# Late weight conversions on ScalarE: first steps kept in the order of the calls, more places for words, two conversions called later

## The chip, the core and the metric

The kernel runs on one core of a Trainium2 chip. Five engines work side by side, each on a queue of its own that it takes in order: PE (TensorE, the matmuls), DVE (VectorE), ACT (ScalarE), POOL (GpSimd) and SP (SyncE, which here issues all DMAs). The metric is the device time of one execution in microseconds (us). Three runs of the kernel before gave 495.65, 496.67 and 497.83; the median is 496.67.

## What is computed

A windowed attention over 2 x 768 tokens (8 heads of 64), a feed-forward block with a softmax-weighted activation and a norm, and a second feed-forward block with ELU:

```python
h = x @ w_in                               # x: attention output, 1536 x 512; w_in 512 x 1024
e = np.exp(h - np.max(h, axis=-1, keepdims=True))
solu = h * e / (np.sum(e, axis=-1, keepdims=True) + 1e-09)
mu, var = solu.mean(-1, keepdims=True), solu.var(-1, keepdims=True)
x = ((solu - mu) / np.sqrt(var + 1e-06) * g_ln) @ w_out

h = x @ w_in2                              # 512 x 2048
g = np.where(h > 0.0, h, np.exp(np.minimum(h, 0.0)) - 1.0)
out = g @ w_out2                           # 2048 x 512
```

The four weights reach the core as 64-bit floats.

## The kernel before

**Conversions.** A weight tile of 128 rows by 512 columns arrives as words (512 KB, 32-bit halves) and is made float32 by `to_f32`: a first step on ACT (line 120, the absolute value of the high halves), one on POOL (line 123), and three on DVE (lines 124, 125 and 129, the last of which also reads the low halves and so frees the place of the words). `convert` adds the split of each number into a high part (ACT, line 133) and a remainder (DVE, line 100), since each product is made of three matmuls on the parts (`mm3x`, lines 103 to 105). The weights w_in2 and w_out2 are the late ones, here called w3 and w4: 16 tiles each, in the order of the list `todo` (w3 0, w3 1, w4 0, w3 2, w3 3, w4 1, w3 4, w3 5, w4 2, w4 3, w3 6, w4 4, w3 7, w4 5, w3 8, w4 6, w3 9, w4 7 ...). A w3 tile stays in SBUF; a w4 tile is split, stored to DRAM (line 364, tensor `w4d`) and loaded again three times as `w4r`. The profile drops the digit of a tensor's name: words of w3 show as `in_w_in`, words of w4 as `in_w_out`, like those of the first block's weights.

**Places for words.** Words lie where results will come later. `y[0..2]`, the output of the first block (512 tokens each), serve as `stage[0..2]`, with two places each: the place h of `stage[2]` is the columns d = 2h and 2h + 1 of `y[2]`. The late words use the two places of `stage[2]` (the list `spare`) until the second call of the first loop over d below, and then four places in tiles `yc` and `yd`, which take over the room of w_in. `fetch` loads words while fewer than len(spare) - 1 are waiting. `more_w` is one late conversion: it calls `fetch`, stores the w4 tile that was converted last, and converts the oldest words.

**Ticks.** After an opening, the work runs in 24 ticks. Tick t issues the scores of query tile t + 6 (`attn_s`), a half row of h (`mm_in`), the transposes of tile t + 4 (`attn_p`), transposes (`tr`) and output products (`mm_out`) of the first block as they come due, and the values of tile t + 3 (`attn_x`: product `x_ps`, then the copy xT on ACT, line 252, and its remainder on DVE). The last `x_ps` is in tick 20. Then come late conversions: one in each of the ticks 11 to 20, two in 21, 22 and 23. `mm_out(i, d)` is the product for third i of the tokens and 128 output columns d; it is copied to y by ACT (line 305), in two pieces where a third crosses two tiles of y. Third 1 (ticks 17 to 20) is the first that writes y[1], third 2 the first that writes y[2]. `lnT` (lines 290 and 100) is the transposed, normalized activation, made from the transposes `t_ps`.

**The turn.** Two loops over d follow, with the products of thirds 2 and 3, the last transposes and more conversions: one in each of the last two calls of the first loop and in each call of the second. Then the second block starts; its first loop makes the remaining conversions. All these products share a PSUM pool of four places (`psb`).

**What sets the order.** SP's queue is in the order of the calls (`manual_schedule`, line 448); before a DMA, it waits until the place it writes is free, and everything called later waits behind it. On the other engines a planner orders the instructions by its own estimate of when each can run, and an instruction whose inputs it takes as landed can be put ahead of earlier calls. `keep_in_program_order` (line 122) forbids this for one instruction: it is queued after the instruction called just before it on its engine. The keyword `pin` of `to_f32` asks for that. In the kernel before, only the conversions of w_out ask for it (line 158).

Of the kernel before, what the change touches and what calls it, by code (L numbers as in the profile page):

```python
# [12 lines left out]
I32 = mybir.dt.int32  # L13
# [38 lines left out]
def tile_kernel(ctx: ExitStack, tc: tile.TileContext, qd, kT, v, w_in, w_out, g_ln, w_in2, w_out2,  # L52
# [4 lines left out]
    state = {"late": 0}  # L57
# [10 lines left out]
    stage = [[t.bitcast(I32)[:, i * 1024:(i + 1) * 1024].rearrange("p (k f) -> p k f", k=KD)  # L68
              for i in range(KD * TC // 1024)] for t in flat]
# [41 lines left out]
    def load_words(bits, src):  # L111
        nc.sync.dma_start(bits, src if len(src.shape) == 3 else src.rearrange("p (k f) -> p k f", k=KD))


    def to_f32(bits, outs=None, pin=False):
        words = bits.rearrange("p k (f two) -> p k f two", two=2)
        low, high = words[:, :, :, 0], words[:, :, :, 1]
        a = p_k.tile([128, KD, 128], I32, tag="conv", name="conv", bufs=3)
        x = a.bitcast(F32)
        first = nc.scalar.activation(x, high.bitcast(F32), AF.Abs)  # L120
        if pin:
            tc.keep_in_program_order(first)
        nc.gpsimd.tensor_scalar(x, x, F64_HUGE, F64_TINY, op0=ALU.min, op1=ALU.max)  # L123
        nc.vector.tensor_scalar(a, a, 3, 0x3FFFFFF8, op0=ALU.logical_shift_left, op1=ALU.bitwise_and)  # L124
        nc.vector.scalar_tensor_tensor(a, high, -0x40000000, a, op0=ALU.bitwise_and, op1=ALU.bitwise_or)
        to = a if outs is None else outs
        if outs is not None:
            low, a = (t.rearrange("p (h k) f -> p h (k f)", h=2) for t in (low, a))
        nc.vector.scalar_tensor_tensor(to, low, 29, a, op0=ALU.logical_shift_right, op1=ALU.bitwise_or)
        return x  # L130

    def split(hi, lo, x):
        nc.scalar.activation(hi, x, AF.Copy)  # L133
        lo_of(lo, x, hi)

    def convert(bits, src, hi, lo, g=None, pin=False):
        if src is not None:
            load_words(bits, src)
        hi, lo = (t if len(t.shape) == 3 else t.rearrange("p (k f) -> p k f", k=KD) for t in (hi, lo))
        x = to_f32(bits, pin=pin)  # L140
        if g is None:
            split(hi, lo, x)
        else:
            nc.scalar.activation(hi, x, AF.Copy, scale=g)
            nc.vector.scalar_tensor_tensor(lo, x, g, hi.bitcast(F32), op0=ALU.mult, op1=ALU.subtract)
# [17 lines left out]
    def load_k(b):  # L163
        k_sb[b] = p_k.tile([128, NP, S + 2 * PAD], F32, tag="k", name="k_sb", bufs=2)
        for p in range(NP):
            nc.sync.dma_start(k_sb[b][:, p, :], kT[b, p])

    def sum_k(b):
        ksum[b] = p_at.tile([128, NP, NB], F32, name="ksum") if b else kws[0][:, :, WIN:KW]
        for p in range(NP):  # L170
            nc.vector.tensor_reduce(
                ksum[b][:, p, :], k_sb[b][:, p, PAD:PAD + S].rearrange("d (n j) -> d n j", j=BLOCK),
                axis=AX.X, op=ALU.max)


    def sum_v(b):
        pst = psb.tile([128, DM], F32, tag="b", name="vs_ps")
        v_sb = p_k.tile([128, NP, S + 2 * PAD], F32, tag="k", name="v_sb", bufs=2).rearrange("p a s -> p (a s)")
        for i in range(S // 128):
            vt = v_sb[:, i * DM:(i + 1) * DM]  # L180
            nc.sync.dma_start(vt, v[b, PAD + i * 128:PAD + (i + 1) * 128, :])
            c0 = NB - i * 4
            nc.tensor.matmul(pst, lhsT=avg[:, c0:c0 + 128], rhs=vt, start=i == 0, stop=i == S // 128 - 1)
        vsum[b] = p_at.tile([128, DM], F32, tag="vsum", name="vsum", bufs=1)
        nc.scalar.activation(vsum[b][WIN:KW, :], pst[WIN:KW, :], AF.Copy)
# [121 lines left out]
                t0 = t1  # L307

    w3t, w3e, w3l, w3_hl, w4s, w4_hl, yhl, yf = {}, {}, {}, {}, {}, {}, {}, {}
    stores, ahead, spare = [], [], [*stage[2]]  # L310
    todo = [("w3", 0), ("w3", 1), ("w4", 0), ("w3", 2), ("w3", 3), ("w4", 1), ("w3", 4), ("w3", 5), ("w4", 2),
            ("w4", 3), ("w3", 6), ("w4", 4), ("w3", 7), ("w4", 5), ("w3", 8), ("w4", 6), ("w3", 9), ("w4", 7),
            ("w4", 8), ("w4", 9), ("w3", 10), ("w3", 11)]
# [3 lines left out]
    def fetch():  # L317
        while todo and len(ahead) < len(spare) - 1:
            what, f = todo.pop(0)
            b = spare[state["late"] % len(spare)]  # L320
            state["late"] += 1
            if what == "w3":
                load_words(b, w_in2[:, f * 128:(f + 1) * 128].bitcast(I32).rearrange("(k p) f -> p k f", p=128))
            else:
                load_words(b, w_out2[f * 128:(f + 1) * 128, :].bitcast(I32))
            ahead.append((what, f, b))

    def home(p):
        if p < 2:
            t = w3t[p] = p_k.tile([128, 3200], F32, tag="k", bufs=2, name="w3f")  # L330
            w4s[p] = t[:, 1792:2816].rearrange("p (c f) -> p c f", c=2)
        elif p == 2:
            w3t[p] = p_k.tile([128, 2048], F32, tag="f2", name="w3f")
        elif p > 4:
            w3t[p] = p_w.tile([128, 2048], F32, tag=f"w{p - 5}", name="w3f")

    def w3f(p):
        return w3t[p][:, :1792].rearrange("p (s f) -> p s f", s=7)

    def base_of(f):  # L340
        return w3f(f // 2)[:, 2:6:3] if f % 2 else w3f(f // 2)[:, 0:4:3]

    def convert_w3(f, b):
        if f % 2 == 0:
            home(f // 2)
        to_f32(b, base_of(f).bitcast(I32))

    def sums_w3(p):
        t = w3f(p)
# [5 lines left out]
    def convert_w4(f, b):  # L355
        t = w4s[f % 2]
        tr_ = t.bitcast(F32R)
        convert(b, None, tr_[:, 0], tr_[:, 1])
        stores.append((f, t))

    def store_w4():
        while stores:
            f, t = stores.pop(0)
            nc.sync.dma_start(w4d[f], t.rearrange("p c f -> p (c f)"))

    def more_w(n=1):
        for _ in range(n):
            fetch()
            store_w4()
            if ahead:  # L370
                what, f, b = ahead.pop(0)
                (convert_w3 if what == "w3" else convert_w4)(f, b)
# [119 lines left out]
    converts = {4: 1, 5: 1, 6: 1, 7: 1, 8: 1, 9: 1, 10: 2}  # L492
    fetches = {2: 1, 3: 1, 4: 1, 5: 1, 6: 1, 7: 1, 8: 1, 9: 1}
    NU = B * NT
    late = {**dict.fromkeys(range(11, 21), 1), 21: 2, 22: 2, 23: 2}
    for t, (j, n) in enumerate(ticks):
        s_n, p_n, x_n = t + LEAD, t + LEAD - 2, t + LEAD - 3
        if t == 0:
            sum_v(1)
        elif t == 1:  # L500
            load_k(1)
        elif t == 3:
            sum_k(1)
        if x_n < NU and t:
            load_v(x_n)
        if s_n < NU:
            for u in (s_n + 1, s_n):
                if u < NU and u not in q_bd:
                    load_q(u)
            load_kw(s_n + 1)  # L510
            attn_s(s_n)
        mm_in(j, n)
        if p_n < NU:
            attn_p(p_n)
        for f, *args in after[t]:
            f(*args)
        if x_n < NU:
            attn_x(x_n)
        for _ in range(fetches.get(t, 0)):
            words.pop(0)()  # L520
        for _ in range(converts.get(t, 0)):
            parts.pop(0)()
        if t == min(late) - 1:
            fetch()
        more_w(late.get(t, 0))
        if x_n == NU - 1:
            p_at.release()
            p_w3 = ctx.enter_context(tc.tile_pool(name="p_w3", bufs=1, side="left", reuse_waits="tile"))
            for f in (3, 4):
                w3t[f] = p_w3.tile([128, 2048], F32, tag=f"f{f}", name="w3f")  # L530
            w3e[0] = p_w3.tile([128, 2, 3, 2, 128], F32R, name="w3e")
            last_t = p_w3.tile([128, 2, KF1, TB], F32R, tag="last", name="lnT")
            lnT_last = [last_t[:, c] for c in range(2)]
    p_in.release()
    p_y = ctx.enter_context(tc.tile_pool(name="p_y", bufs=1, side="right", reuse_waits="tile"))
    tb = [p_y.tile([128, 2, KD, 256], I32, tag=n, name="bits") for n in ("yc", "yd")]
    for d in range(KD):
        mm_out(NJ // 3 - 2, d)
        more_w(d > 1)
        if d == 1:  # L540
            spare[:] = [t[:, c] for c in range(2) for t in tb]
            state["late"] = 0
            fetch()
        if d == 2:
            split_y(0)
            mids = [stage[0][h].bitcast(F32).rearrange("p k f -> p (k f)")[:, c * TC:(c + 1) * TC]
                    for h in range(2) for c in range(2)]
        if d < 3:
            tr(NJ - 3 + d)
# [210 lines left out]
```

## Time and profile before

| | us |
|---|---|
| median of three runs | 496.67 |
| profiled execution, its own time | 498.08 |
| its span | 496.30 |
| PE busy | 469.2 (95%) |
| DVE busy | 330.3 (67%) |
| ACT busy | 288.2 (58%) |
| POOL busy | 125.5 (25%) |

All durations below come from the profiled execution, and times of day are counted from the start of its span. Matmuls overlap, so the busy time of PE is that in which at least one is running. A granted clock of 1.00 is the upper of the two levels that the rows show. An idle time before an instruction stands in brackets with what ended it.

### The profile page before, as it was taken

The page shows a single profiled execution, that of the slowest core. Times are in us where ns is not written, and L with a number is a line of the kernel's source. Part 1 is how long each engine was busy: PE and PEld are TensorE (multiplying, and loading weights), DVE is VectorE, ACT ScalarE, POOL GpSimd, SP SyncE. Part 2 cuts the span into 40 slices and gives each one's busy share as a digit, 9 for nine tenths or more (in the row PEclk, how much of TensorE's full clock was granted, in tenths as well). Part 3 has the DMA queues.
Part 4 walks back from the last instruction along what each step waited for, and adds up shares of the span by engine and source line. Part 5 has one row for each costly group of instructions (what it writes and reads, how often), then busy time and mean ns, then how long its engine had stood idle before and what let it go on. Part 6 is the DMA issues. An engine that isn't in the chain of part 4 may idle for free.

```text
span 496.3 us, 7444 instructions
## 1 busy us (share of the span) xinstructions
PE 469.2 (95%) x2568; PEld 391.9 (79%) x2568; DVE 330.3 (67%) x759; ACT 288.2 (58%) x635; POOL 125.5 (25%) x198
## 2 busy tenths in 40 slices
PE   0979999999998999889999999999999999999996
PEld 0655788889987898789888888888888888887885
DVE  3698969898659467979899998267755565541000
ACT  1675789976567356645773766367776666660001
POOL 2787465874442421222314200000000000000000
PEclk9999999999998999989999999999999999999999
DMA  8994996161481541377859662332122212128564
GB/s 276 345 355 143 267 301 185 56 197 48 151 237 44 176 160 53 130 245 261 297 170 314 237 213 85 128 127 84 44 85 86 77 52 81 47 95 276 180 197 142
DMA packets 40117, 82.47 MB, mean 166 GB/s; under 512 B 9616, under 2 KB 18448, under 8 KB 40080
## 3 DMA queue, kind: packets, MB, share of 16 engines
q1 hardware_dynamic: 40080, 82.00, 50.4%
q8 instruction: 20, 0.33, 0.3%
q14 instruction: 17, 0.14, 0.1%
HBM read 70.46 MB, written 11.53 MB: 165 GB/s over the span
## 4 chain that ended last, share of the span: by engine, by line
PE 81%; DVE 6%; DMA 5%; ACT 3%; POOL 2%; issue 1%; SPq 0%; POOLq 0%; ACTq 0%
PE o_ps L103 8%; PE o_ps L105 8%; PE o_ps L104 8%; PE h L103 7%; PE h L105 7%; PE h L104 6%; PE c L105 5%; PE c L103 5%; PE c L104 5%; PE y_ps L103 4%; PE y_ps L105 4%; PE y_ps L104 4%; PE s_ps L213 3%; DMA y<-in_w_out 3%; PE x_ps L249 2%; DMA k_sb<-in_kT 1%
## 5 line engine op out<-in xcount | busy, mean ns | idle before, releaser
L123 POOL TENSOR_SCALAR conv<-conv 128x512 f32<-128x512 f32 x48 | 40.5, 846 | 85.4 <-ACT conv L120 76.8
L227 POOL TENSOR_SCALAR sm<-sm,st 128x120 f32<-128x120 f32 x96 | 47.3, 510 | 24.1 <-DVE st L225 15.4
L103 PE MATMUL o_ps<-w4r,g_hl 128*128 128x512 f32 x128 | 49.8, 389 | 0.0
L104 PE MATMUL o_ps<-w4r,g_hl 128*128 128x512 f32 x128 | 49.8, 389 | 0.0
L103 PE MATMUL y_ps<-lnT,w_out 128*128 128x384 f32 x128 | 45.4, 354 | 3.2 <-DVE lnT L100 3.0
L105 PE MATMUL o_ps<-w4r,g_hl 128*128 128x512 f32 x128 | 45.6, 389 | 0.0
L104 PE MATMUL y_ps<-lnT,w_out 128*128 128x384 f32 x128 | 44.5, 348 | 0.0
L105 PE MATMUL y_ps<-lnT,w_out 128*128 128x384 f32 x128 | 44.3, 348 | 0.0
L103 PE MATMUL h<-w_in,xT 128*128 128x512 f32 x96 | 40.3, 420 | 1.6 <-ACT xT L252 1.6
L213 PE MATMUL s_ps<-kw,q_bd 128*128 128x120 f32 x192 | 28.7, 296 | 13.2 <-POOL kw L96 12.4
L120 ACT ACTIVATE conv<-y 128x512 f32<-128x512 f32 x32 | 21.5, 675 | 31.5 <-DMA y<-in_w_in 23.7
L105 PE MATMUL h<-w_in,xT 128*128 128x512 f32 x96 | 38.6, 402 | 0.5 <-DVE xT L100 0.5
L104 PE MATMUL h<-w_in,xT 128*128 128x512 f32 x96 | 38.2, 398 | 0.6 <-DVE w_in L100 0.6
L222 ACT ACTIVATE sm<-sm,st 128x120 f32<-128x120 f32 x96 | 36.7, 387 | 3.5 <-DVE st L219 3.0
L213 PEld LDWEIGHTS s_ps<-kw,q_bd 128*128 128x128 f32 x192 | 25.1, 203 | 14.6 <-POOL kw L96 12.3
L600 DVE COPY y<-o_ps 128x512 f32<-128x512 f32 x5 | 3.4, 690 | 43.9 <-PE o_ps L105 43.2
L572 ACT ACTIVATE y<-y 128x512 f32<-128x512 f32 x48 | 30.1, 629 | 0.8
L124 DVE TENSOR_SCALAR conv<-conv 128x512 int32<-128x512 int32 x48 | 22.4, 467 | 11.4 <-POOL conv L123 11.4
L602 ACT ACTIVATE y<-o_ps 128x512 f32<-128x512 f32 x6 | 3.6, 599 | 44.9 <-PE o_ps L105 44.9
L100 DVE TENSOR_TENSOR g_hl<-y,g_hl 128x512 fp32r<-128x512 f32 x32 | 22.4, 700 | 9.3 <-ACT g_hl L133 9.3
L103 PEld LDWEIGHTS y_ps<-lnT,w_out 128*128 128x128 f32 x128 | 25.0, 195 | 4.0 <-DVE lnT L100 3.3
L103 PEld LDWEIGHTS o_ps<-w4r,g_hl 128*128 128x128 f32 x128 | 24.0, 188 | 5.1
(146 smaller groups left out, 1270.8 us busy)
## 6 DMA issues: line engine op xcount, KB each, us to landing
w4r<-w4d SPq DMA_DIRECT2D x48, 512.0 KB, 4.1
y<-in_w_in SPq DMA_DIRECT2D x17, 512.0 KB, 6.6
w4d<-w3f SPq DMA_DIRECT2D x16, 512.0 KB, 3.0
y<-in_w_out SPq DMA_DIRECT2D x15, 512.0 KB, 5.2
q_bd<-in_qd SPq DMA_DIRECT2D x24, 256.0 KB, 6.1
vw<-in_v SPq DMA_DIRECT2D x24, 192.0 KB, 5.2
bits<-in_w_out SPq DMA_DIRECT2D x9, 512.0 KB, 6.2
bits<-in_w_in SPq DMA_DIRECT2D x7, 512.0 KB, 4.3
```

What stands on the lines that cost most here:

```text
L100: nc.vector.tensor_tensor(out_, x, hi.bitcast(F32), op=ALU.subtract)
L103: nc.tensor.matmul(ps, lhsT=l[0][ls], rhs=r[0][rs], start=first, stop=False, skip_group_check=parts)
L104: nc.tensor.matmul(ps, lhsT=l[0][ls], rhs=r[1][rs], start=False, stop=False, skip_group_check=parts)
L105: nc.tensor.matmul(ps, lhsT=l[1][ls], rhs=r[0][rs], start=False, stop=last, skip_group_check=parts)
L120: first = nc.scalar.activation(x, high.bitcast(F32), AF.Abs)
L123: nc.gpsimd.tensor_scalar(x, x, F64_HUGE, F64_TINY, op0=ALU.min, op1=ALU.max)
L124: nc.vector.tensor_scalar(a, a, 3, 0x3FFFFFF8, op0=ALU.logical_shift_left, op1=ALU.bitwise_and)
L213: nc.tensor.matmul(sps[:, p, 0:KW], lhsT=q_bd[n][:, p, :], rhs=kw[:, p, :], start=True, stop=True)
L222: nc.scalar.activation(sm[:, p, :], sm[:, p, :], AF.Exp, bias=nm[:, p:p + 1], scale=-1.0, accum_out=ss[:, p:p + 1])
L227: nc.gpsimd.tensor_scalar(sm[:, p, :], sm[:, p, :], ri[:, p:p + 1], 1.0, op0=ALU.mult, op1=ALU.mult)
L249: nc.tensor.matmul(xps[ds, p, :], lhsT=vw[:KW, p * 128 + hh * D:p * 128 + (hh + 1) * D], rhs=pT[:KW, p, hh * TQ:(hh + 1) * TQ], start=True ...
L572: nc.scalar.activation(m, m, AF.Exp, scale=-1.0)
```

## The change

- The first step of every w3 and w4 conversion is pinned, as that of w_out is already.
- `spare` starts with the four places of `stage[1]` and `stage[2]`, so that up to three words are fetched ahead, from tick 10 on; at tick 14 it goes back to the two places of `stage[2]`.
- Ticks 22 and 23 make one conversion each instead of two. The four places in `yc` and `yd` are taken, and fetched into, before the first loop over d instead of after its second call, and each of the loop's four calls makes one conversion instead of only the last two. Eighteen conversions are called by the end of this loop, before and after. The last words in `y[2]` are w3 7 and w4 5, where they were w3 8 and w4 6.

```diff
-    stores, ahead, spare = [], [], [*stage[2]]
+    stores, ahead, spare = [], [], [*stage[1], *stage[2]]
...
     def convert_w3(f, b):
         if f % 2 == 0:
             home(f // 2)
-        to_f32(b, base_of(f).bitcast(I32))
+        to_f32(b, base_of(f).bitcast(I32), pin=True)
...
     def convert_w4(f, b):
         t = w4s[f % 2]
         tr_ = t.bitcast(F32R)
-        convert(b, None, tr_[:, 0], tr_[:, 1])
+        convert(b, None, tr_[:, 0], tr_[:, 1], pin=True)
         stores.append((f, t))
...
-    late = {**dict.fromkeys(range(11, 21), 1), 21: 2, 22: 2, 23: 2}
+    late = {**dict.fromkeys(range(11, 21), 1), 21: 2, 22: 1, 23: 1}
...
         if t == min(late) - 1:
             fetch()
+        if t == 14:
+            spare[:] = stage[2]
         more_w(late.get(t, 0))
...
     tb = [p_y.tile([128, 2, KD, 256], I32, tag=n, name="bits") for n in ("yc", "yd")]
+    spare[:] = [t[:, c] for c in range(2) for t in tb]
+    fetch()
     for d in range(KD):
         mm_out(NJ // 3 - 2, d)
-        more_w(d > 1)
-        if d == 1:
-            spare[:] = [t[:, c] for c in range(2) for t in tb]
-            state["late"] = 0
-            fetch()
+        more_w()
```

## Rows read from the trace of the kernel before

**Rows 1.** The page, busy time of each engine over the span.

```profile
PE 469.2 (95%) x2568; PEld 391.9 (79%) x2568; DVE 330.3 (67%) x759; ACT 288.2 (58%) x635; POOL 125.5 (25%) x198
```

**Rows 2.** Windows: stretch, its length, busy PE, PEld, DVE, ACT, POOL; clock, DMA share, GB/s.

```profile
110.00:146.00 36.00, 36.00 (x254) 31.92 (x253) 25.04 (x84) 23.25 (x63) 16.61 (x30) 1.00 0.53 160
146.00:162.00 16.00, 14.18 (x103) 12.12 (x102) 13.54 (x44) 10.92 (x31) 4.40 (x7) 0.89 0.16 48
162.00:187.00 25.00, 25.00 (x184) 22.25 (x182) 12.98 (x29) 10.32 (x23) 8.20 (x14) 1.00 0.55 174
...
198.00:220.00 22.00, 18.10 (x102) 17.31 (x101) 17.67 (x31) 11.27 (x22) 5.46 (x6) 0.92 0.45 154
220.00:300.00 80.00, 80.00 (x381) 69.77 (x380) 75.91 (x126) 51.84 (x89) 18.76 (x17) 1.00 0.71 247
```

**Rows 3.** Waits of PE from 140 to 165: us in total, times, longest.

```profile
PE h L103 <- ACT xT L252: 0.8, 1, 0.8
PE p_ps L232 <- DVE st L224: 0.6, 1, 0.6
```

**Rows 4.** Waits of PE from 195 to 230.

```profile
PE y_ps L103 <- DVE lnT L100: 3.0, 1, 3.0
PE t_ps L288 <- ACT y L305: 0.9, 1, 0.9
```

**Rows 5.** Timeline of ACT, ticks 13 to 16: start, duration, instruction, idle before it.

```profile
126.93 0.68 ACT L120 ACTIVATE conv<-y 128x512 f32<-128x512 f32 x1 [0.80 <-DMA y<-in_w_out]
...
133.04 0.38 ACT L252 ACTIVATE xT<-x_ps 128x256 fp32r<-128x256 f32 x1
...
148.26 0.69 ACT L120 ACTIVATE conv<-y 128x512 f32<-128x512 f32 x1 [1.12 <-DMA y<-in_w_out]
148.86 0.58 ACT L290 ACTIVATE lnT<-t_ps 128x512 fp32r<-128x512 f32 x1
...
154.33 0.37 ACT L252 ACTIVATE xT<-x_ps 128x256 fp32r<-128x256 f32 x1
```

**Rows 6.** Timeline of DVE, 149 to 159.

```profile
149.47 0.69 DVE L100 TENSOR_TENSOR lnT<-t_ps,lnT 128x512 fp32r<-128x512 f32 x1 [1.59 <-ACT lnT L290]
...
158.03 0.68 DVE L129 SCALAR_TENSOR_TENSOR conv<-y,conv 128x512 int32<-128x512 int32 x1
```

**Rows 7.** Timeline of ACT, 206 to 219.

```profile
206.96 0.70 ACT L120 ACTIVATE conv<-y 128x512 f32<-128x512 f32 x1 [1.60 <-DMA y<-in_w_out]
...
208.93 1.09 ACT L290 ACTIVATE lnT<-t_ps 128x512 fp32r<-128x512 f32 x2
213.33 0.68 ACT L120 ACTIVATE conv<-y 128x512 f32<-128x512 f32 x1 [3.31 <-DMA y<-in_w_in]
...
218.57 0.44 ACT L305 ACTIVATE y<-y_ps 128x128 f32<-128x128 f32 x2
```

**Rows 8.** Timeline of DVE, last step on w3 7 and on w3 8.

```profile
208.89 0.69 DVE L129 SCALAR_TENSOR_TENSOR w3f<-y,conv 128x512 int32<-128x512 int32 x1
...
216.36 0.69 DVE L129 SCALAR_TENSOR_TENSOR w3f<-y,conv 128x512 int32<-128x512 int32 x1
```

**Rows 9.** Timeline of SP's queue: stores of w4 0 and w4 1, k of tile 22.

```profile
135.31 0.34 SPq L364 DMA_DIRECT2D w4d<-w3f  x1
...
137.00 0.48 SPq L198 DMA_DIRECT2D kw<-in_kT  x1
...
161.46 0.33 SPq L364 DMA_DIRECT2D w4d<-w3f  x1
```

**Rows 10.** Tile kw, the load issued at 137.00: from issue to landing.

```profile
DMA to landing us min/median/max: 4.4/4.4/4.4
```

**Rows 11.** Timeline of PE: scores of tile 22, values of tile 21 (tick 18).

```profile
148.89 1.15 PE L213 MATMUL s_ps<-kw,q_bd 128*128 128x120 f32 x8
...
170.60 0.69 PE L249 MATMUL x_ps<-pT,vw 120*64 120x64 f32 x16
```

## Prediction

> **What bounds the kernel now.** I read the page's busy shares first, then a table of the stretches between the phases, then the waits of the two stretches in which TensorE (PE) loses time, and last the queues of ScalarE (ACT), VectorE (DVE) and SyncE (SP) in those two.
>
> The busy line says that PE is the bound: 469.2 us of a span of 496.3 [rows 1]. An average hides where the rest goes, so I cut the span by phase. PE is busy without a hole and at full clock from 110 to 146, from 162 to 187 and from 220 to 300 us; no engine's saving in these stretches can shorten the kernel. Two stretches lose. From 146 to 162 PE is busy 14.18 of 16.00 us at a granted clock of 0.89; from 198 to 220 it is busy 18.10 of 22.00 at 0.92 [rows 2]. Waiting is 1.82 and 3.90 us. The clock has two levels, 1.2 and 2.4 GHz, so a mean of 0.89 over 16 us means 16 x 0.11 = 1.76 us lost, and 22 x 0.08 is again 1.76. The first stretch loses 3.58 us, the second 5.66, together **9.24 us**. That is the most that this change can give: it touches neither the start, where the first steps of the earlier weights are in order already, nor the last 200 us, which hold no late conversion.
>
> Next, what ended these waits. In the first stretch PE waits 0.8 us for ACT's copy xT and 0.6 for a DVE step (the rest of the 1.82 is in waits of 0.2) [rows 3]; in the second 3.0 us for DVE's lnT and 0.9 for ACT's copy into y [rows 4]. None of these names a conversion. The ACT queue shows what came before: at 148.26 the first step of a late conversion (line 120) sat at the head of the queue for 1.12 us until its words landed, then took 0.69, and the lnT copy at 148.86 and the xT copy behind it went late [rows 5]. DVE, which needs that lnT copy, was idle for 1.59 us until 149.47 [rows 6], and then worked without a gap to 162. The second stretch shows the same at 206.96 (1.60 us of waiting for words, then 0.70), with lnT behind it at 208.93, and at 213.33 (3.31 us) [rows 7].
>
> There is a second cause in 198 to 220. The PSUM pool of these products has four places. The copies of products d=0 and d=1 of third 2 into y[2] run only at 218.57 [rows 7], because the words of w3 8 lie in those columns of y[2] until DVE's last step on them, which starts at 216.36 [rows 8]. Two of four places are held until then, and PE must wait for lnT to free one of the other two.
>
> **The change part by part.** Nothing is computed more or less: 32 conversions with the same ACT, POOL and DVE instructions. What moves is when.
>
> *The pin.* Each first step now stands behind the ACT instruction called before it; in ticks 11 to 20 this is xT of its tick. One tick has one xT, and the last (tick 20) follows the last x_ps product, so ticks can be counted back. The step that ran at 148.26 belongs to tick 16, whose xT ran at 154.33: it goes back by about 6 us. Its words landed by 148.2, so it waits for nothing then. Removed from in front of lnT are 1.12 + 0.60 us (to the start of lnT at 148.86). DVE's idle 1.59 us closes, and w4 1's DVE steps, the last of which stood at 158.03 [rows 6], move behind the steps on which PE waited. PE's single waits there are 0.8 us or less, so 1.6 us of advance covers each of them; the clock is below 1.00 in the two stretches with waits and in no other [rows 2], so I let it go with them. Of 3.58 us I take **3.3**, bounds 0 and 3.58; near the upper end, because the advance is double the longest wait.
>
> *More places, up to tick 14.* Three words are fetched at tick 10 instead of one; y[1] is written only from tick 17, after its last word (tick 15) is read. Cost on PE nothing: the pinned steps cover it, as words now land a tick or more before use. If that cover were gone, a step would hold ACT as the one at 148.26 does, for 1.12 us.
>
> *Two conversions to the turn.* w3 8 and w4 6 leave tick 23 and use the freed space of w_in. So y[2] d=0 is held by w3 7 and not by w3 8: its last DVE step starts at 208.89 and not at 216.36 [rows 8]. The copies of d=0 and d=1 can follow at about 209.6, and with 0.4 us for one of them PE gets its place at about 210.0 instead of 211.6. That shortens the 3.0 us wait by 1.5, and the 0.9 us wait for the copy into y goes away. The low clock I leave standing, since 1.82 us of waiting in the first stretch brought 1.76 us of it. So **2.4** of 5.66, bounds 0 and 5.66: if lnT also comes sooner nothing is left, and if words are late as before nothing is won. I take the middle, because the row on w3 7 supports the smaller gain alone.
>
> *What a later conversion pushes on SP.* SP's queue is in the order of the calls, and a store of finished w4 words stands in it ahead of later loads of q, k, v. The w4 0 store was issued at 135.31 and the k window of tile 22 at 137.00, 1.69 behind it [rows 9]. Its first step ran at 126.93; pinned behind xT of tick 13 (133.04) it starts at 133.4 [rows 5]. From first step to store took 126.93 to 135.31, 8.4 us, for w4 0 and 148.26 to 161.46, 13.2 us, for w4 1. With 8.4 the store is issued at 141.8 and the window, at 4.4 us to land [rows 10], is there at 147.9; the product needs it at 148.89 [rows 11]. That is 1.0 us of cover where there were 7.5. With 13.2 PE would wait 3.8. DVE is less loaded around 133 to 142 than where the 13.2 were taken (25.04 of 36.00 us against 13.54 of 16.00 [rows 2]), so I sit near 8.4 and charge **0.5**, bounds 0 and 3.8.
>
> Sum: 3.3 + 2.4 - 0.5 = 5.2 us. The profiled run took 498.08 (span 496.30 and 1.78 around it), so 492.9 by its own time; that run lies 1.41 above the median of the runs, 496.67, and against the median the sum is **491.5**.
>
> **The rivals.**
>
> *All of it.* Both stretches close: 496.67 - 9.24 = 487.4. For it: both have the same visible cause. Against it: w3 7 still holds y[2] until 209.6, and DVE has no gap from 149.5 to 162.
>
> *The wait moves to the last places.* From tick 16 on a word is fetched only in the call that converts it, into one of two places, each freed by the conversion two before, which is now a tick later. Tick 21 has two conversions, and ticks 21 to 23 take PE only 11 us. If a word lands after the place of its pin, ACT stands at it as it did at 206.96 and 213.33 (1.60 and 3.31 us), and lnT or a copy into y stands behind. Then the second stretch stays as it is and 3.3 remain: 493.4. The Trainium skill, Perfetto Trace Analysis, section Tensor Engine Instruction, says that ACT, DVE and GPSIMD queues are strict FIFO, so a place in the order gives no cover by itself. The trace agrees: lnT at 208.93 came after the step at 206.96 and not before it.
>
> *The stores hold SP (slower).* If w4 0 takes the 13.2 us of w4 1, the window of tile 22 lands at 152.7: PE waits 3.8, and 1.76 of low clock come with it as in the first stretch. w4 1, pinned at 154.7, would be stored at 167.9, the v window behind it (0.4 to issue, 4.4 to land) is there at 172.7, and x_ps needs it at 170.60 [rows 11]: 2.1 more. With 3.58 won and nothing in the second stretch, 496.67 - 3.58 + 3.8 + 1.76 + 2.1 = 500.8. It decides from 9.4 us for w4 0 (148.89 - 4.4 - 1.69 - 133.4). Against it: the planner sees the same queue and can put other products ahead of the late one.
>
> *The pin binds nothing.* If the steps already stood there in the order, or another instruction takes the head of ACT and waits instead, the time stays at 496.7. Against it stands the 6 us between the step at 148.26 and its xT.
>
> **How the numbers follow.** Forecast 491.5 with 0.45, all of it (487.4) 0.12, the last places (493.4) 0.20, the stores (500.8) 0.13, nothing 0.10. What a measurement of this kernel can tell from no change is about 0.5%, 2.5 us, so faster means under 494.2 and slower over 499.2. Faster gets the forecast but for 0.04, all of the second, and 0.10 of the third, together 0.63. Slower gets the stores and 0.02 of the third case, if the moved wait is longer than the old one: 0.15. Same has the other 0.22. The range goes from the floor at 487.4 to 497.8: it takes in the first three cases and that of no change, and leaves out the stores and the worst of the third.
>
> **What would show it.** Right: no DMA wait of line 120 between 140 and 160, PE without a hole from 60 to the turn and a clock of 1.00 in the first stretch; copies into y[2] some 8 us earlier, no wait of t_ps for y. Wrong: s_ps of tile 22 waiting for k or q behind a store (the stores), or ACT waits on words of w3 7 to w4 6 with lnT behind them and PE's wait for lnT still 3 us or more (the last places). The forecast fails altogether if the two waits of PE come back behind other releasers, that is, if DVE and not ACT's order set them.

## The result and the profile after

The kernel after takes 489.87 us at the median (489.54 to 490.29, 4 runs), the kernel before 496.16 (494.97 to 497.83, 4 runs): a ratio of 0.9846, 95% interval 0.9818 to 0.9875. The forecast was 491.5; the gain is 6.3 us where 5.2 was worked out. The profiled execution took 490.29 us with a span of 488.5, against 498.08 and 496.3, so 7.8 us of span have to be found in the rows.

The page of the kernel after: busy time of each engine over the span. The work is what it was [rows 1]; PE's time falls by 4.0 us with the same 2568 instructions.

```profile
PE 465.2 (95%) x2568; PEld 388.7 (80%) x2568; DVE 330.8 (68%) x759; ACT 286.4 (59%) x635; POOL 123.8 (25%) x198
```

The windows of after, in the columns of [rows 2]: stretch, its length, busy PE, PEld, DVE, ACT, POOL; clock, DMA share, GB/s.

```profile
146.00:162.00 16.00, 14.78 (x126) 12.84 (x125) 13.94 (x45) 11.55 (x34) 8.26 (x14) 1.00 0.29 85
...
198.00:220.00 22.00, 20.92 (x127) 20.61 (x126) 17.10 (x31) 11.98 (x25) 5.34 (x7) 1.00 0.59 200
220.00:300.00 80.00, 79.94 (x369) 67.87 (x368) 76.26 (x128) 50.65 (x87) 15.17 (x16) 1.00 0.73 248
```

The first stretch lost 1.82 us of waiting and 1.76 of clock; now it loses 1.22 and none: 2.36 back. The second lost 3.90 and 1.76; now it loses 1.08 and none: 4.58 back. Together 6.94 of the 7.8; most of the rest was already there before either stretch (the xT of tick 13 runs at 132.45 and not at 133.04). The waits of PE from 140 to 165 and from 195 to 230, in the columns of [rows 3, 4], are one each:

```profile
PE h L103 <- ACT xT L252: 1.2, 1, 1.2
PE y_ps L103 <- DVE lnT L100: 1.1, 1, 1.1
```

The timeline of ACT in ticks 13 to 16 and around 201 to 214 shows the new order (start, duration, instruction, idle before it and its releaser):

```profile
132.45 0.38 ACT L252 ACTIVATE xT<-x_ps 128x256 fp32r<-128x256 f32 x1
132.73 0.67 ACT L120 ACTIVATE conv<-y 128x512 f32<-128x512 f32 x1
...
148.87 0.38 ACT L252 ACTIVATE xT<-x_ps 128x256 fp32r<-128x256 f32 x1 [1.43 <-PE x_ps L249]
149.15 0.66 ACT L120 ACTIVATE conv<-y 128x512 f32<-128x512 f32 x1
...
153.76 0.38 ACT L252 ACTIVATE xT<-x_ps 128x256 fp32r<-128x256 f32 x1
154.02 0.67 ACT L120 ACTIVATE conv<-y 128x512 f32<-128x512 f32 x1
...
204.85 0.60 ACT L290 ACTIVATE lnT<-t_ps 128x512 fp32r<-128x512 f32 x1
...
205.87 0.59 ACT L290 ACTIVATE lnT<-t_ps 128x512 fp32r<-128x512 f32 x1
207.72 0.45 ACT L305 ACTIVATE y<-y_ps 128x128 f32<-128x128 f32 x2 [1.26 <-DVE w3f L129]
...
211.27 1.09 ACT L290 ACTIVATE lnT<-t_ps 128x512 fp32r<-128x512 f32 x2
...
214.06 0.67 ACT L120 ACTIVATE conv<-y 128x512 f32<-128x512 f32 x1 [0.66 <-DMA y<-in_w_out]
```

Each first step (line 120) now stands right behind the xT of its tick and waits for no words there, where the one of tick 16 waited 1.12 us with lnT behind it [rows 5]. The copies of d=0 and d=1 into y[2] run at 207.72 and not at 218.57 [rows 7], 10.85 us earlier: DVE's last step on w3 7 releases them, and w3 8 is no longer in y[2]. Both lnT copies at 211.27 run before ACT comes to the words of w4 5 at 214.06.

DVE, first its lnT step that answers to the one of [rows 6], then its last step on w3 7, which answers to [rows 8]; and PE, the scores of tile 22, the product after the wait for xT and the one after the wait for lnT:

```profile
147.48 0.69 DVE L100 TENSOR_TENSOR lnT<-t_ps,lnT 128x512 fp32r<-128x512 f32 x1 [0.77 <-ACT lnT L290]
...
206.20 1.42 DVE L129 SCALAR_TENSOR_TENSOR w3f<-y,conv 128x512 int32<-128x512 int32 x1
```

```profile
148.75 1.15 PE L213 MATMUL s_ps<-kw,q_bd 128*128 128x120 f32 x8
...
154.19 0.50 PE L103 MATMUL h<-w_in,xT 128*128 128x512 f32 x1 [1.22 <-ACT xT L252]
...
206.34 0.44 PE L103 MATMUL y_ps<-lnT,w_out 128*128 128x384 f32 x1 [1.08 <-DVE lnT L100]
```

That lnT step comes 1.99 us earlier than in the kernel before, and DVE is idle for 0.77 us in front of it instead of 1.59. The xT of tick 16 is only 0.57 us earlier (153.76, 154.33 before), no more than the 0.59 by which the xT of tick 13 was early already.

SP's queue, as in [rows 9]: the store of w4 0, the k window of tile 22, the store of w4 1.

```profile
139.50 0.34 SPq L364 DMA_DIRECT2D w4d<-w3f  x1
...
141.18 0.49 SPq L198 DMA_DIRECT2D kw<-in_kT  x1
...
161.50 0.33 SPq L364 DMA_DIRECT2D w4d<-w3f  x1
```

The store of w4 0 is 4.2 us later than before, the one of w4 1 isn't, and no product waits for k, q or v.

### The profile page after: what moved, and what is told of

The parts are those of the page before. It is cut to its first block, busy times and chain, and to the rows that moved or that the text cites. A ratio compares the mean times of both kernels' runs of the same rounds, so it can differ in the third digit from the quotient of the medians.

```text
span 488.5 us, 7446 instructions
## 1 busy us (share of the span) xinstructions
PE 465.2 (95%) x2568; PEld 388.7 (80%) x2568; DVE 330.8 (68%) x759; ACT 286.4 (59%) x635; POOL 123.8 (25%) x198
## 4 chain that ended last, share of the span: by engine, by line
PE 70%; DVE 12%; DMA 6%; ACT 4%; issue 3%; POOL 2%; SPq 0%; POOLq 0%; ACTq 0%; DVEq 0%
PE o_ps L105 8%; PE o_ps L104 7%; PE o_ps L103 7%; PE c L105 5%; PE c L103 5%; PE c L104 5%; PE h L103 5%; PE h L105 5%; PE h L104 5%; PE s_ps L213 4%; PE x_ps L249 3%; PE y_ps L103 3%; PE y_ps L105 3%; PE y_ps L104 3%; DMA bits<-in_w_out 2%
## 5 line engine op out<-in xcount | busy, mean ns | idle before, releaser
L123 POOL TENSOR_SCALAR conv<-conv 128x512 f32<-128x512 f32 x48 | 37.6, 785 | 95.3 <-ACT conv L120 94.0
L227 POOL TENSOR_SCALAR sm<-sm,st 128x120 f32<-128x120 f32 x96 | 48.7, 525 | 22.6 <-DVE st L225 8.6
L103 PE MATMUL y_ps<-lnT,w_out 128*128 128x384 f32 x128 | 43.8, 342 | 1.1 <-DVE lnT L100 1.1
L104 PE MATMUL y_ps<-lnT,w_out 128*128 128x384 f32 x128 | 43.2, 337 | 0.0
L105 PE MATMUL y_ps<-lnT,w_out 128*128 128x384 f32 x128 | 43.1, 338 | 0.0
L120 ACT ACTIVATE conv<-y 128x512 f32<-128x512 f32 x30 | 20.3, 677 | 13.9 <-DMA y<-in_w_in 12.4
L105 PEld LDWEIGHTS o_ps<-w4r,g_hl 128*128 128x128 f32 x128 | 23.9, 188 | 5.4 <-DVE g_hl L100 0.5
L103 PEld LDWEIGHTS o_ps<-w4r,g_hl 128*128 128x128 f32 x128 | 24.0, 188 | 5.2 <-ACT g_hl L133 0.2
L104 PEld LDWEIGHTS o_ps<-w4r,g_hl 128*128 128x128 f32 x128 | 24.0, 188 | 5.0
```

The lines of the kernel that those rows point to most:

```text
L103: nc.tensor.matmul(ps, lhsT=l[0][ls], rhs=r[0][rs], start=first, stop=False, skip_group_check=parts)
L104: nc.tensor.matmul(ps, lhsT=l[0][ls], rhs=r[1][rs], start=False, stop=False, skip_group_check=parts)
L105: nc.tensor.matmul(ps, lhsT=l[1][ls], rhs=r[0][rs], start=False, stop=last, skip_group_check=parts)
L227: nc.gpsimd.tensor_scalar(sm[:, p, :], sm[:, p, :], ri[:, p:p + 1], 1.0, op0=ALU.mult, op1=ALU.mult)
```

## The experiments

The kernel before was run beside every series: 496.63 in the first (25 runs), 496.83 in the second (13), 496.82 in the third (11). Parts of the change are called pin, places and turn; the functions named stand in the diff ahead of the prediction.

### The three parts by themselves

**The pin alone.**

```
-        to_f32(b, base_of(f).bitcast(I32))
+        to_f32(b, base_of(f).bitcast(I32), pin=True)
...
-        convert(b, None, tr_[:, 0], tr_[:, 1])
+        convert(b, None, tr_[:, 0], tr_[:, 1], pin=True)
```

> Only the pin of the late first steps, on the kernel before. Theory 'two causes': the pin cures the first stretch (146 to 162), where a first step stood before lnT, and the turn cures the second (198 to 220), where words of w3 8 hold y[2]. So the first stretch loses 1.2 us or less of waiting at a clock of 1.00 (3.58 us before) and the second still 4 us or more (5.66 before): 2 to 4 us faster than before, about 493. Rival 'ACT alone': both stretches come from ACT standing at words, so the pin gives all of it: about 490. Rival 'places': with two places words land after the pinned step, ACT stands at it again, within 1.5 us of before.

Measured: 498.85 us, ratio 1.004 (1.0015 to 1.0064). Slower. The part to which the prediction gave the largest gain costs 2.2 us by itself. (Its profiled execution took 2639.54 us, and its trace isn't read; the pin was profiled once more, below.)

**The further places alone.**

```
-    stores, ahead, spare = [], [], [*stage[2]]
+    stores, ahead, spare = [], [], [*stage[1], *stage[2]]
...
+        if t == 14:
+            spare[:] = stage[2]
```

> Only the two further places up to tick 14, on the kernel before. Theory 'two causes': the step that stands before lnT at 148.26 is that of w4 1 (tick 16), which has no place ahead, and its load stays behind the same queue; no difference from before that can be told (within 1.5 us), first stretch still losing 3 us or more. Rival 'places': words that land earlier are enough by themselves, the step no longer waits: 3 us or more faster.

Measured: 493.50, ratio 0.993 (0.9904 to 0.9957), so 3.1 us gained by what was costed at nothing. The first stretch of its trace, as a row of the windows:

```profile
146.00:162.00 16.00, 15.87 (x130) 13.34 (x128) 14.66 (x44) 11.07 (x33) 8.78 (x17) 1.00 0.46 140
```

Only 0.13 us are lost there. With no pin the planner puts a step where its words are expected, and with two more places they come sooner: the store of w4 0 is issued at 130.13 (135.31 before [rows 9]), the words of w4 1 are asked for at 134.12, and the steps at 140.65 and 144.43 wait for no DMA. So the late word of the first stretch has two cures: come later to the step, or fetch sooner. The second stretch still loses 3.01 us.

**The turn alone.**

```
-    late = {**dict.fromkeys(range(11, 21), 1), 21: 2, 22: 2, 23: 2}
+    late = {**dict.fromkeys(range(11, 21), 1), 21: 2, 22: 1, 23: 1}
...
+    spare[:] = [t[:, c] for c in range(2) for t in tb]
+    fetch()
     for d in range(KD):
         mm_out(NJ // 3 - 2, d)
-        more_w(d > 1)
...
+        more_w()
```

> Only the two conversions moved to the turn, with places in yc and yd from its start, on the kernel before. Theory 'two causes': the second stretch gets PE's places in PSUM back sooner, as w3 7 and not w3 8 holds y[2]: 3 to 5 us faster than before, about 492, with the copies into y[2] of d=0 and 1 at about 210 and not 218.6, and the first stretch losing 3.5 us as before. Rival 'ACT alone': the same wait for lnT stays, within 1.5 us of before.

Measured: 493.48, ratio 0.9933 (0.9903 to 0.9963). The windows of its trace:

```profile
146.00:162.00 16.00, 13.96 (x122) 11.58 (x120) 13.17 (x44) 11.45 (x33) 3.46 (x7) 1.00 0.15 47
...
198.00:220.00 22.00, 20.12 (x123) 19.78 (x122) 20.64 (x36) 13.07 (x27) 6.72 (x8) 1.00 0.62 218
```

The second stretch loses 1.88 instead of 5.66. The first loses 2.04 of waiting, more than before, and yet its clock is 1.00: the 1.76 us of clock, which the prediction tied to the 1.82 us of waiting, don't follow from them.

### The parts in pairs

**Pin and turn**, the change without the further places (the two diffs above):

```
-        to_f32(b, base_of(f).bitcast(I32))
+        to_f32(b, base_of(f).bitcast(I32), pin=True)
...
+    late = {**dict.fromkeys(range(11, 21), 1), 21: 2, 22: 1, 23: 1}
```

> Pin and turn without the further places (two places in ticks 10 to 23). Theory 'two causes': the further places give nothing that the pin doesn't: within 1.5 us of the changed kernel, about 490. Rival 'places': without words ahead the pinned steps wait for theirs and ACT stands: 2 us or more slower than the changed kernel, waits of line 120 for words between 110 and 160.

Measured: 490.12 (489.86 to 490.39), ratio 0.987 (0.9821 to 0.9918); its windows and its two waits are those of the whole change (1.2 for xT, 1.1 for lnT). Beside the pin the places give 0.2 us, less than the interval: the zero holds there.

**Pin and places** was run together with two repetitions: the pin alone, with its edit above, and the kernel before, with none.

```
+    stores, ahead, spare = [], [], [*stage[1], *stage[2]]
...
+        to_f32(b, base_of(f).bitcast(I32), pin=True)
```

> Pin and further places, without the turn. Theory 'held places': the further places end at tick 14 and leave the second stretch as with the pin alone: within 1.5 us of 498.9. Rival 'late words': what makes the pin alone slow is words that land late, and words fetched ahead mend it: 494 or less.

> The pin alone once more, for a profile that can be read. It took 498.85 where the kernel before took 496.63. Theory 'held places': the first stretch is cured (1.3 us of waiting or less, clock 1.00), and the second is worse than before, since the steps of w3 8 and w4 6, now pinned behind the last ACT step of tick 23, keep y[2] longer: copies into y[2] of d=0 and 1 after 221 (218.6 before), PE waiting 6 us or more. Rival 'late words': ACT stands at words in the first stretch too, which loses as before.

> The kernel before, unchanged, profiled once more. The turn alone waited 2.04 us in the first stretch with the clock at 1.00, where the kernel before waited 1.82 at 0.89. Theory 'clock by chance': the fall of the clock does not follow from a wait of some 2 us every time, so this profile can show the same waits (1.8 and 3.9 us, within 0.3) with a clock of 1.00 in one stretch or both, and a span shorter by 1.8 us for each. Rival 'clock by the wait': the same waits and 0.89 and 0.92 again, span within 0.7 us of 496.3.

Measured: pin and places 499.65, ratio 1.0043 (1.0019 to 1.0066), as the pin alone; the pin again 499.22; before again 498.51 (one run each). The pin's trace: the windows of both stretches, then, for the second, the waits of PE from 195 to 230, ACT, and two of PE's waits by themselves.

```profile
146.00:162.00 16.00, 14.78 (x126) 12.85 (x125) 14.14 (x45) 11.58 (x34) 8.19 (x15) 1.00 0.39 125
...
198.00:220.00 22.00, 15.99 (x89) 15.21 (x88) 16.14 (x30) 9.75 (x19) 4.98 (x6) 0.87 0.52 176
```

```profile
PE y_ps L103 <- DVE lnT L100: 4.6, 2, 3.6
PE y_ps L103 <- ACT y L305: 1.7, 1, 1.7
PE t_ps L288 <- DVE lnT L100: 1.4, 1, 1.4
```

```profile
211.40 0.60 ACT L290 ACTIVATE lnT<-t_ps 128x512 fp32r<-128x512 f32 x1
215.08 0.66 ACT L120 ACTIVATE conv<-y 128x512 f32<-128x512 f32 x1 [3.08 <-DMA y<-in_w_out]
215.64 0.58 ACT L290 ACTIVATE lnT<-t_ps 128x512 fp32r<-128x512 f32 x1
...
224.65 0.43 ACT L305 ACTIVATE y<-y_ps 128x128 f32<-128x128 f32 x2
```

```profile
206.50 0.44 PE L103 MATMUL y_ps<-lnT,w_out 128*128 128x384 f32 x1 [1.03 <-DVE lnT L100]
...
217.00 0.69 PE L103 MATMUL y_ps<-lnT,w_out 128*128 128x384 f32 x1 [3.56 <-DVE lnT L100]
```

The first stretch loses 1.22 us at a clock of 1.00, just as in the kernel after. In the second, the wait until 206.50 is the one that the kernel after has too; the others are new.

They are the rival in which the wait moves to the last places, and worse than it was priced. ACT stands 3.08 us at the words of w4 5 with an lnT behind it at 215.64, and PE waits 3.56 us, until 217.00, for DVE's step on that lnT. The strict order that the Trainium skill states (Perfetto Trace Analysis, Tensor Engine Instruction) is seen once more: the lnT starts as the step's successor, never past it. And w3 8, pinned later, now holds y[2] and two PSUM places until 224.65 instead of 218.57.

Before again loses 1.30 us in the first stretch and 3.97 in the second, both at a clock of 1.00, and it loses more behind them (rows of its windows):

```profile
146.00:162.00 16.00, 14.70 (x125) 12.33 (x124) 14.39 (x46) 11.98 (x34) 4.71 (x8) 1.00 0.18 59
...
198.00:220.00 22.00, 18.03 (x110) 17.46 (x110) 18.24 (x34) 10.71 (x23) 4.84 (x6) 1.00 0.55 185
220.00:300.00 80.00, 77.71 (x358) 66.77 (x357) 72.55 (x122) 49.70 (x85) 18.02 (x16) 0.98 0.69 239
```

The waits of the second stretch repeat. The low clock is not in these two stretches; it comes once, later, at 0.50 from 270 to 272 us. Just before, PE had waited 2.29 us, until 268.74, for a tile that ACT split at 267.99, right behind a first step that stood 3.68 us at its words. In the trace of [rows 2] the same step stood 3.32 us, until 267.95, and PE waited for nothing (80.00 of 80.00). So the span of before again, 496.7, is not shorter for the better clock in the two stretches, as its expectation had it: what the kernel before loses moves from one execution to the next.

**Places and turn**, the change without the pin:

```
+    stores, ahead, spare = [], [], [*stage[1], *stage[2]]
...
+    late = {**dict.fromkeys(range(11, 21), 1), 21: 2, 22: 1, 23: 1}
```

> Further places and turn, without the pin. Theory 'two ways to the first stretch': the places alone cured the first stretch (0.13 us of waiting) and the turn most of the second, each 3 us, so both together give 490 to 491, as with pin and turn. Rival 'the pin is needed': without it ACT stands at words in the second stretch, and the time stays at 492.5 or more.

Measured: 490.77 (490.02 to 493.31), ratio 0.9856 (0.9807 to 0.9905); in its trace 0.13 us are lost in the first stretch and 2.74 in the second, at 1.00. The medians side by side:

| | without turn | with turn |
|---|---|---|
| neither | 496.6 to 496.8 | 493.48 |
| places | 493.50 | 490.77 |
| pin | 498.85 | 490.12 |
| pin and places | 499.65 | 489.87 |

The turn is worth 2.7 to 3.2 us without the pin and 8.7 to 9.8 with it. The pin costs 2.2 and 6.2 without the turn and gains 3.4 and 0.9 with it (the 0.9 is not clear of the spread of places and turn, 490.02 to 493.31). So the parts don't add, and something that the turn takes away must stand between the pin and its gain.

### What the turn takes away: held PSUM places, or late words

Two things go with the turn: w3 8 leaves y[2], which frees two of four PSUM places, and two conversions leave the end of tick 23, which thins the words. To part them, the copies of third 2 that go to the columns of y[2] with the words of w3 8 in them were sent to a scratch tile, all words and conversions left where they are in the calls. These two kernels so leave the results of third 2 out of those columns of y[2].

```
-                nc.scalar.activation(y[t0 // TC][:, d, t0 % TC:t0 % TC + t1 - t0],
-                                     ys[d][:, t0 - i * TB:t1 - i * TB], AF.Copy)
+                to = dump[:, :t1 - t0] if i == 2 and t0 // TC == 2 else y[t0 // TC][:, d, t0 % TC:t0 % TC + t1 - t0]
+                nc.scalar.activation(to, ys[d][:, t0 - i * TB:t1 - i * TB], AF.Copy)
+                if i == 3 and t0 // TC == 2:
+                    nc.scalar.activation(y[2][:, d, :128], ys[d][:, :128], AF.Copy)
```

In the kernel before:

> The kernel before, with one change: the copies of the product of third 2 that go to the first 128 columns of y[2], where the words of w3 8 lie, go to a scratch tile of the same size instead, and the product of third 3 writes those columns later (so the output is not the reference's in the part of y[2]; the ACT work is the same but for four copies of 128 columns after 220 us). No PSUM place is then held until the last step on w3 8. Theory held places: the wait of y_ps for lnT of 3 to 3.6 us that the kernel before has in its second stretch falls to 1.5 or less, 2 to 4 us less in all, 492.5 to 495. Rival late words (ACT stands at words with lnT behind it, and held places cost nothing): the wait stays, 496.8 as before.

In the pin alone:

> The pin alone, with the same change to the copies into y[2] (output not the reference's there). With the pin alone the kernel took 498.9, and PE waited 4.6 us for lnT while ACT stood 3.08 us at the words of w4 5 and two PSUM places were held until 224.6. Held places: both lnT copies run before ACT comes to the late step, PE's wait for lnT is 1.5 us or less, the second stretch is busy at least 20 of 22 us at a clock of 1.00, and the time is 489 to 492, as with pin and turn together. Late words: the step of w4 5 still waits about 3 us with an lnT behind it, and the time stays within 1.5 of 498.9.

Measured: 491.16 (490.99 to 491.66), ratio 0.9879 (0.9846 to 0.9912), for the kernel before with free places; 488.85 (488.79 to 489.35), ratio 0.983 (0.9792 to 0.9869), for the pin with them. The second is 10.0 us below the pin alone and no slower than the whole change (489.70 in the same series), with no turn in it. Its second stretch and that of the kernel before with free places, in this order (the first has no wait of PE from 195 to 230):

```profile
198.00:220.00 22.00, 22.00 (x135) 21.90 (x135) 18.79 (x35) 12.36 (x28) 4.65 (x6) 1.00 0.54 188
```

```profile
198.00:220.00 22.00, 21.34 (x130) 21.01 (x129) 17.40 (x32) 11.47 (x26) 4.86 (x6) 1.00 0.56 189
```

And ACT in the kernel before with free places, at the words of w4 5, w3 8 and w4 6:

```profile
204.88 0.69 ACT L120 ACTIVATE conv<-y 128x512 f32<-128x512 f32 x1 [1.64 <-DMA y<-in_w_out]
...
211.24 0.69 ACT L120 ACTIVATE conv<-y 128x512 f32<-128x512 f32 x1 [2.81 <-DMA y<-in_w_in]
...
212.78 1.09 ACT L290 ACTIVATE lnT<-t_ps 128x512 fp32r<-128x512 f32 x2
...
218.36 0.66 ACT L120 ACTIVATE conv<-y 128x512 f32<-128x512 f32 x1 [3.45 <-DMA y<-in_w_out]
```

The words are about as late as before: ACT stands 1.64 us at those of w4 5 and 2.81 at those of w3 8, where [rows 7] have 1.60 and 3.31, and 3.45 at those of w4 6. PE waits 0.66 us in this stretch (until 207.06, for a copy of ACT behind the step at 204.88) and 0.74 just before it. With four places PE has products to go on with while ACT stands; with two it doesn't. With the pin, too, the words of w4 5 come hardly sooner (their step runs at 214.47, and at 215.08 in the pin alone), but both lnT copies have run by then. Late words alone cost 0.7 us in this stretch and nothing with the pin; held places, by the medians, cost 5.7 us in the kernel before and 10.0 with the pin, waits and low clock together. The Trainium skill (Perfetto Trace Analysis, Optimization Strategy) says that the same gap, repeating on the engine that should be saturated, can mean that SBUF or PSUM is too small for the next tile. Here four places are enough, and two of them were kept by a copy that waited for SBUF columns. The gain in the kernel before was larger than the 2 to 4 us expected, because the 0.9 us wait for a copy into y went too [rows 4], and because its clock stayed up (0.999 to 1.000 in all four runs).

### A version that joins the two cures of the first stretch

What the kernel after still loses in the first stretch is 1.22 us of waiting for xT. The pin put its own step (149.15, 0.66 us) into a stretch of ACT that then has no gap until that xT at 153.76. So the pin was kept from tick 17 on only, with places and turn as in the kernel after.

```
-        to_f32(b, base_of(f).bitcast(I32), pin=True)
+        to_f32(b, base_of(f).bitcast(I32), pin=state["pin"])
...
-        convert(b, None, tr_[:, 0], tr_[:, 1], pin=True)
+        convert(b, None, tr_[:, 0], tr_[:, 1], pin=state["pin"])
...
+        state["pin"] = t > 16
         more_w(late.get(t, 0))
```

> The kernel after, with the pin only from tick 17 on; the steps of ticks 11 to 16 are left to the planner as they are with places and turn. What is left in the kernel after is 1.22 us of waiting for xT in the first stretch (14.78 of 16.00 busy) and 1.08 for lnT in the second; places and turn without the pin had 15.87 of 16.00 in the first. If the two cures add, the first stretch gains 1.1 us and the time is 488.8; if the wait for xT only moves to a later tick, it stays within 0.5 of the kernel after (489.9).

> The kernel after, unchanged, on the chip of this series: 489.9 within 0.7, 6.0 to 7.5 less than the kernel before, and the same two waits of PE (xT 1.2, lnT 1.1) at a clock of 1.00 in both stretches.

Measured: 488.91 (488.09 to 490.16, 6 runs) against 489.70 (489.27 to 490.37, 6 runs) for the kernel after, unchanged; ratios to before 0.9835 (0.9806 to 0.9864) and 0.985 (0.9823 to 0.9877). The first stretch of the version:

```profile
146.00:162.00 16.00, 15.74 (x132) 13.76 (x131) 10.02 (x37) 10.62 (x33) 6.98 (x15) 1.00 0.28 92
```

The loss there falls from 1.22 to 0.26, so the two cures add in the trace. The median is where the adding of the cures put it (488.8), 0.8 us below the kernel after, but the runs overlap; in time the version is not told apart from the kernel after.

## Why the prediction was right, and where its steps were not

**Where the time is lost: right.** In the pair of traces the two stretches of [rows 2] changed and nothing else did much, and their waits shrank to one each.

**The pin, 3.3: mis-sized, and it doesn't stand alone.** Most of what was to be seen was seen: no step at a DMA between 140 and 160, lnT no longer behind one, a clock of 1.00. PE without a hole was not: the wait for xT is still there, 1.22 us. And 1.76 of the 3.58 was clock, and before again shows the same stretch with 1.30 us of waiting and none of clock. Measured against that, the pin left 1.22, a gain of 0.1; against the profiled execution of [rows 2], 2.36. Two steps failed. One let the clock go with the waits (and took, in the other terms, that 1.82 us of waiting bring 1.76 of clock). The other had 1.6 us of advance cover each wait: lnT gained 1.99 us, but the xT that PE waits for, that of tick 16, gained none of it, since its product was there at 151.84 and ACT came to it at 153.76. The waits of 0.6 and 0.2 us went, and the one for this xT grew from 0.79 to 1.22, because ACT's work moved in front of it and did not go away. Beside the turn the pin does gain 3.4 us, near the 3.3, but not there alone: against the turn by itself the first stretch loses 1.22 and not 2.04, the second 1.07 and not 1.88.

**The turn, 2.4: mis-sized; 4.58 in the pair of traces, and not all of it the turn's.** By itself the turn does what the term says: the copies of d=0 and d=1 run at 208.94, PE goes on at 209.26 with the place of one of them, after 1.88 us instead of 3.0, t_ps has no wait for y, and the stretch loses 1.88 us instead of 5.66. In the whole change the 3.0 us wait ends in another way. PE goes on at 206.34, before DVE's last step on w3 7 is through (206.20, 1.42 long) and before the copies at 207.72; what came sooner is lnT, and the pin alone has this same wait (1.03 until 206.50). The term names that only as its upper bound ("if lnT also comes sooner nothing is left"). What the turn takes away there are the waits that follow in the pin alone: 1.42, 3.56 and 1.68 us. And the clock was left standing at 0.92; it is 1.00.

**The sum of the terms: near by errors that partly cancel, so in part by luck.** In the traces the first term came out 0.9 too large, the second 2.2 and SP's charge 0.5 the other way. The terms were added as if each had its own stretch. The runs show that the pin without the turn makes the second stretch worse (15.99 of 22.00 busy, against 18.03 in before again). The prediction names both halves of the cause, words at which ACT stands and two places held, but prices them apart. That the standing costs 0.7 us or nothing in this stretch once the places are free is what the two runs with free places showed.

**More places, 0: right beside the pin, wrong by itself.** Pin and turn alone give the result; without the pin the places gain 3.1.

**SP, 0.5: it cost nothing.** From first step to store w4 0 took 132.73 to 139.50, 6.8 us, below the 8.4 that was taken and far from the 13.2 of the bound. For w4 1 it took 154.02 to 161.50, 7.5 us, where 13.2 were taken. The k window, issued at 141.18, landed 4.8 us later at 146.0, and the scores of tile 22 ran at 148.75, 2.8 us after that and 0.14 before their time in [rows 11]; the prediction had left 1.0 us of cover. The slower rival falls with that, and without its own counter: the planner had no need to put other products ahead.

**The other rivals.** All of it (487.4) came nearer than expected: 2.30 of the two stretches' 9.24 us are left. The wait that moves to the last places didn't come with the whole change but does with the pin alone, at 498.85 and not at 493.4. That the pin binds nothing falls with ACT's order in after: the step of tick 16 runs at 154.02, right behind its xT, and not at 148.26.

## What to carry to other kernels

When two causes meet in one stretch, price them together: here a queue that stood at its head cost the bound engine only the time for which that engine had nothing else to go on with. So count the free buffers at that moment before you cost the stall. Look for buffers that are kept by a consumer which waits for something unrelated, here PSUM kept by a copy waiting for SBUF columns; to free them gave 5.7 us, where fetching the late words sooner gave 3.1 and pinning their steps lost 2.2. And look at two executions of the kernel before, if they can be had, before a term is built on a low clock seen in one.

## What the runs showed of the hardware

**The low clock moves about, and in these runs it costs less than its share.** The 49 runs of the kernel before that stood beside the experiments, by the mean granted clock over the span:

| mean clock | runs | median us | lowest and highest |
|---|---|---|---|
| 1.000 | 5 | 496.1 | 495.33 to 496.83 |
| 0.995 to 0.997 | 28 | 496.4 | 494.63 to 500.04 |
| 0.991 to 0.993 | 16 | 497.4 | 495.87 to 500.55 |

By its share a mean of 0.992 over 496 us would cost 4.0 us, of which 0.7 lie behind the last matmul in the trace of [rows 2] (PE is done at 492.5, and the clock falls after 494); the medians differ by 1.3, between groups whose runs overlap. That waits take up part of the difference (words land by their own time, and a slower PE reaches them later) fits this, but it was not tried by itself. The Trainium skill (TensorE: Matmul & The Clock Gate, section What's actually happening) says of a kernel's start that the count of slow matmuls differs from run to run of the same kernel; no run here was read for its start. In mid-kernel the traces show the like: 0.50 from 158 to 160 and from 212 to 214 us in one execution of the kernel before, from 270 to 272 in the other, each time behind waits of PE (1.82 in all, 3.04 and 2.29 us), while the turn alone waited 2.04 us in the first stretch and stayed at 1.00. In the kernel after, with waits of 1.22 and 1.08 us, both stretches are at 1.00 and the means of the runs at 0.998 to 1.000. In the pin alone, with its wait of 3.6 us, nine of ten runs and the repetition are at 0.993 to 0.997.

**The spread shrinks, for a reason that stays open.** The kernel before spreads over 4.4 to 5.4 us in a series, the kernel after over 0.8 and 1.1. The longest waits don't explain that: the pin alone, which has them, spreads over 1.5 in nine runs.
